# Moving every third VectorE score product to GpSimd, with a longer exponential ring and another rule for TensorE fillers

## The chip, the cores and the metric

The kernel runs on one core of one Trainium2 chip. The metric is the device time of one launch in microseconds. Before the change, five runs had a median of 813.22 us (809.14, 813.22, 813.22, 816.80 and 820.69). All of that is one launch on one core; there is no traffic between cores.

## What is computed

Two attention blocks read the same input and are mixed by a gate. A is a linear attention with a softmax feature map, B is an ordinary softmax attention:

```python
def _A_ref(x, wqkv, w_phi, wo):            # B, S, D = 1, 2048, 512; H = 32; Dh = 16
    q, k, v = heads(x @ wqkv)
    pq = einsum("bhsd,hdf->bhsf", q, w_phi)
    pk = einsum("bhsd,hdf->bhsf", k, w_phi)
    phi_q = concatenate([softmax(pq), softmax(-pq)], -1)
    phi_k = concatenate([softmax(pk), softmax(-pk)], -1)
    kv, z = einsum("bhsf,bhsd->bhfd", phi_k, v), phi_k.sum(2)
    num, den = einsum("bhqf,bhfd->bhqd", phi_q, kv), einsum("bhqf,bhf->bhq", phi_q, z)
    return merge(num / (den[..., None] + 1e-6)) @ wo

def _B_ref(x, wqkv, wo):
    q, k, v = heads(x @ wqkv)
    p = softmax(einsum("bhqd,bhkd->bhqk", q, k) * Dh ** -0.5)
    return merge(einsum("bhqk,bhkd->bhqd", p, v)) @ wo

g = sigmoid((x * gate_w).sum(-1, keepdims=True))
out = g * _A_ref(x, ...) + (1 - g) * _B_ref(x, ...)
```

(`heads` and `merge` stand for the reshapes and transposes of the reference.) Block B needs the exponential of 32 x 2048 x 2048 scores. Cut into tiles of 128 keys by 512 queries, that is 2048 tiles, and nearly everything in this kernel is arranged around them.

## The kernel before, in words

**Tiles and blocks.** A tile is named (b, i, kt): b is one of 32 blocks (four chunks of 512 queries times eight groups of heads), i one of the block's four heads, kt one of sixteen stretches of 128 keys. A score tile is one matmul with a contraction of 32 rows (`qk_mm`); up to four of different heads can lie side by side in the array. Its exponentials multiply the values in another matmul (`pv_mm`) that adds into `psO`, one PSUM bank for the four heads of the block. At a block's end VectorE transposes `psO` (T1), divides by the row sums, and every second block transposes back (T2) into the input of the output projection.

**Two ways to an exponential.** Most tiles go to ScalarE. `slots` pairs them into slots of three and two tiles by turns; slot j is read from one half of `psS` by one ACTIVATE (`add_exp`, line 756) and written to one place of the ring `Ebuf`, which has `ERING = 7` places. The list `DN` says how many tiles of each block go to VectorE instead: 392 of the 2048 before the change, in 98 groups of four. For a group, each tile is computed into a free PSUM bank (`dq`), VectorE converts it to a bit pattern (D1, line 733), then for the whole group of 2048 columns D2 takes the mantissa bits into a buffer m (line 743), D3 the exponent bits into a buffer s (line 745), and D4 multiplies the pattern t by m in place (line 747). TensorE then adds two terms per tile into `psO`, from s and from t (`add_pvd`). The buffers t and s come from small rings (`rings`; before: t has four late ones, x0, x1, a0, a1, s three), and m is a single buffer, so the next group's D2 must wait until this group's product has been read out of m.

**What GpSimd does before.** Apart from setting up masks in the first 14 us, GpSimd only multiplies the feature maps of block A (`phi`, line 946): 32 instructions of 128 x 1024.

**The order.** Nothing is ordered by hand. Every operation is an `Op` with an engine, a duration, a priority and dependencies. `Plan.layout` plays the five engines forward with those durations and at each step gives a free engine the ready operation with the lowest priority number; `Plan.emit` writes each engine's list in that order, with semaphore waits for the dependencies between engines. On the chip each engine follows its list; durations and priorities have no other effect. One rule of the planner matters here: an operation marked `lock` isn't started while a locked operation of the other one of VectorE and GpSimd is under way in the plan (D2, D3, D4, the block-end product and `phi` are locked). That is a rule of the plan alone: no semaphore carries it, so on the chip the two may still overlap if one of them runs late.

**Free banks.** `psM` (bank M) and the sixth bank of `psS` (S5) are lent for one use at a time to projections, `dq` tiles and transposes (`fill`), and come free when the result has been read (`drain`).

**Fillers.** `layout` also puts matmuls without use on TensorE to keep it busy: up to two in front of a score slot (line 688, `op.room`; only where the slot before has three tiles), when a running `debt` exceeds a bound, and single ones into bank M when nothing else is ready (`P.idle`, line 1078).

**Pace of block A.** Its work carries priorities that rise with slot numbers: 76 + 8 per key tile, 210 + 12 per query tile.

Of the kernel before, what the change touches and what calls it, by code (L numbers as in the profile page):

```python
# [10 lines left out]
ALU = mybir.AluOpType  # L11
# [17 lines left out]
DN = (0, 6, 12, 12, 7, 10, 10, 4, 10, 13, 14, 9, 10, 10, 16, 7, 13, 14, 15, 9, 16, 17, 12, 17, 13, 21, 12, 21, 14, 19, 10, 19)  # L29
G_EARLY = 8  # L30
D_FIRST = 12
RIDE = 0.02
PE_CLASS = {"qk": 0, "dq": 0, "pv": 1, "term": 1}
T_PRIO = -10.0
G_DEEP = 5
D_AHEAD = 20.0
CONT = -60.0
ERING = 7
# [5 lines left out]
class Op:  # L44
    __slots__ = ("eng", "dur", "prio", "fn", "deps", "succ", "nd", "ready", "end", "lat", "sem", "count",
                 "name", "full", "extra", "room", "fill", "bank_of", "acq", "rel", "seq", "clock", "take", "pos", "margin", "done", "kind", "heads", "lock")

    def __init__(self, eng, dur, prio, fn, name):
# [7 lines left out]
        self.full, self.extra, self.room, self.fill = 0.0, 0, 0, False  # L56
# [22 lines left out]
class Plan:  # L79
# [3 lines left out]
    def __init__(self):  # L83
        self.ops = []
        self.writer, self.readers = {}, {}
        self.idle, self.rate, self.inslot = None, 0.57, 0.12
# [37 lines left out]
    def layout(self):  # L124
# [14 lines left out]
        debt, debt_t = 0.0, 0.0  # L139
# [3 lines left out]
        while left:  # L143
# [28 lines left out]
            for e in ENGINES:  # L172
# [45 lines left out]
                if e == "pe":  # L218
                    debt, debt_t = min(debt + self.rate * (t - debt_t), 0.5), t
                if pick is None and e == "pe" and self.idle is not None and debt > self.idle[1]:  # L220
                    b, _, fn, after = self.idle
                    if b.free and b.shared and all(x.done for x in after):
                        pick = Op("pe", 0.22, 1e9, fn, "idle")
                        pick.seq, pick.deps, pick.nd = len(self.ops), list(after), 0
                        pick.full = 0.21
                        pick.acq = pick.rel = Fill([b])
                        pick.acq.bank = b
# [12 lines left out]
                if e == "pe":  # L240
                    busy_next = any(o.fill and (o.acq is None or any(b.free and b.shared for b in o.acq.banks))
                                    for _, _, o in queues[e])
                    if op.room and not busy_next and debt > self.inslot and t > 60.0:
                        op.extra = 2 if op.room > 1 and debt > self.inslot + 0.21 else 1
                        op.full += 0.21 * op.extra
                        op.dur += 0.105 + 0.215 * op.extra
                    debt = max(debt - op.full, -0.2)
# [94 lines left out]
def _build(ctx, nc, A_x, A_wqkv, A_w_phi, A_wo, B_wqkv, B_wo, gate_w, out):  # L342
# [23 lines left out]
    Ebuf = sb([128, ERING + 1, 1536], name="E")  # L366
# [145 lines left out]
    def drain(f, mm, eng, dur, prio, fn, reads=(), writes=(), name="", last=True, after=()):  # L512
        op = P.add(eng, dur, prio, lambda e: fn(e, f.ap()), reads=reads, writes=writes, after=[mm] + list(after),
# [9 lines left out]
    kv_mm, va_free = [], []  # L523
# [518 lines left out]
    for t in range(KT):  # L1042
        wp_fill(1, t, 66.0 + t)
# [69 lines left out]
```

## Time and profile before

| What | Value |
| --- | --- |
| median of five runs | 813.22 us |
| the profiled execution's own time | 809.14 us |
| its span, first to last instruction | 807.3 us |
| ScalarE (ACT) busy | 786.4 us, 97% |
| TensorE (PE) busy | 732.1 us, 91% |
| VectorE (DVE) busy | 686.6 us, 85% |
| GpSimd (POOL) busy | 78.1 us, 10% |
| exponentials of block B (line 756) | 663, in two shapes: 331 of 1536 columns, 331 of 1024, one of 512 |
| mean granted TensorE clock | 0.992 |

The shares are averages over the whole span. Busy time of ScalarE counts overlapping records once: an exponential of 1536 columns has a record of 1563 ns and one of 1024 columns a record of 1142 ns, but one follows the other at shorter distance. The VectorE load isn't even. In stretches of 20 us from 60 us on it lies between 10.8 us (200 to 220 us) and 19.8 us (300 to 320 us, 580 to 600 us), and from 440 us to 760 us it is never under 17.1 us.

The profiled execution is the fastest of the five runs; the median lies 4.1 us above it.

### The profile page before, as it was taken

To read this page: it belongs to the slowest core of one execution; us is meant where nothing else is said; L and a number is where in the kernel's file an instruction comes from. 1 tells how busy PE (TensorE), PEld (TensorE's weight loads), DVE (VectorE), ACT (ScalarE), POOL (GpSimd) and SP (SyncE) were. 2 spreads that over 40 slices of the span, in tenths; PEclk is the share of its full clock that TensorE was granted. 3 is DMA by queue.
4 is the path that set the end of the run, shared out by engine and by line. 5 is a ranking of instruction groups with operands and counts; after the bars stand their busy time and mean duration, and the time that the engine had idled before them with its cause. 6 is when DMAs were issued, how large, how long until landed. Compare 5 with 4: busy or idle time off the path is not lost.

```text
span 807.3 us, 13768 instructions
## 1 busy us (share of the span) xinstructions
PE 732.1 (91%) x5821; PEld 232.3 (29%) x5893; DVE 686.6 (85%) x1110; ACT 786.4 (97%) x734; POOL 78.1 (10%) x60
## 2 busy tenths in 40 slices
PE   9899999999998898998899888899898888888999
PEld 4332332333232222233232222222222222222223
DVE  3478877887668999888988999989899999999895
ACT  6999999999999999999999999999999999999995
POOL 5000002132340003000302000000000000000000
PEclk9899999999999999999999999999999999999999
DMA  6600000000100000000000000000000000000000
GB/s 126 137 2 1 1 2 1 1 1 1 53 2 1 1 7 1 7 14 2 1 1 2 1 1 2 1 20 7 1 1 1 1 2 1 1 1 1 20 8 27
DMA packets 18957, 9.29 MB, mean 12 GB/s; under 512 B 13264, under 2 KB 18896, under 8 KB 18896
## 3 DMA queue, kind: packets, MB, share of 16 engines
q1 hardware_dynamic: 17408, 7.74, 4.0%
q8 instruction: 46, 0.75, 0.4%
q10 hardware_dynamic: 1104, 0.66, 0.3%
q0 software_dynamic: 384, 0.02, 0.1%
q14 instruction: 15, 0.12, 0.1%
HBM read 3.69 MB, written 2.10 MB: 7 GB/s over the span
## 4 chain that ended last, share of the span: by engine, by line
ACT 83%; PE 11%; DVE 5%; issue 1%
ACT E_t L756 80%; PE psS L671 3%; ACT EA_t L937 3%; PE psO L769 3%; PE psS L520 2%; PE psM L520 2%; DVE vA_t L733 1%; DVE Tx_t L733 1%; PE psM L440 1%; DVE stat_t L942 1%; DVE vA_t L747 1%; DVE vA_t L745 1%; PE psM L1078 0%; DVE WB_t L743 0%; DVE qz_t L587 0%
## 5 line engine op out<-in xcount | busy, mean ns | idle before, releaser
L756 ACT ACTIVATE E_t<-psS 128x1536 bf16<-128x1536 f32 (+1 forms) x663 | 759.3, 1352 | 6.1 <-PE psS L671 5.0
L671 PE MATMUL psS<-qz_t,kTB_t 32*128 32x512 bf16 x1871 | 284.3, 388 | 53.2 <-ACT E_t L756 42.4
L769 PE MATMUL psO<-E_t,vaug_t 128*32 128x512 bf16 (+1 forms) x1656 | 249.2, 394 | 0.0
L671 PEld LDWEIGHTS psS<-qz_t,kTB_t 32*128 32x128 bf16 x1871 | 70.9, 91 | 272.2 <-ACT E_t L756 209.9
L769 PEld LDWEIGHTS psO<-E_t,vaug_t 128*32 128x32 bf16 (+1 forms) x1656 | 59.0, 93 | 135.5 <-issue 130.4
L733 DVE TENSOR_SCALAR Tx_t<-psS 128x512 int16<-128x512 f32 x118 | 80.5, 682 | 20.0 <-PE psS L671 15.7
L769 PE MATMUL psO<-vA_t,vaug_t 128*32 128x512 bf16 (+1 forms) x384 | 93.3, 391 | 0.0
L671 PE MATMUL psM<-qz_t,kTB_t 32*128 32x512 bf16 x177 | 68.3, 386 | 1.0 <-ACT EA_t L937 0.3
L733 DVE TENSOR_SCALAR Tx_t<-psM 128x512 int16<-128x512 f32 x90 | 61.2, 680 | 9.2 <-PE psM L671 6.0
L733 DVE TENSOR_SCALAR vA_t<-psS 128x512 int16<-128x512 f32 x88 | 60.1, 683 | 10.2 <-PE psS L671 7.6
L769 PE MATMUL psO<-Tx_t,vaug_t 128*32 128x512 bf16 (+1 forms) x208 | 59.5, 386 | 0.0
L946 POOL TENSOR_TENSOR phiQ_t<-EA_t,stat_t 128x1024 bf16<-128x1024 bf16 x16 | 32.9, 2056 | 262.4 <-DVE stat_t L944 251.9
L733 DVE TENSOR_SCALAR vA_t<-psM 128x512 int16<-128x512 f32 x76 | 52.0, 684 | 3.7 <-PE psM L671 2.3
L942 DVE TENSOR_REDUCE stat_t<-EA_t 128x64 f32<-128x1024 bf16 x32 | 38.8, 1213 | 15.7 <-ACT EA_t L937 15.5
L946 POOL TENSOR_TENSOR phiK_t<-EA_t,stat_t 128x1024 bf16<-128x1024 bf16 x16 | 33.3, 2087 | 186.9 <-DVE stat_t L944 179.4
L747 DVE TENSOR_TENSOR Tx_t<-Tx_t,WB_t 128x2048 bf16<-128x2048 bf16 x42 | 50.8, 1209 | 0.1
L747 DVE TENSOR_TENSOR vA_t<-vA_t,WB_t 128x2048 bf16<-128x2048 bf16 x41 | 49.7, 1213 | 0.1
L769 PE MATMUL psO<-WB_t,vaug_t 128*32 128x512 bf16 (+1 forms) x112 | 32.2, 388 | 0.0
L688 PE MATMUL psS<-xT_t,ident_t 128*128 128x512 bf16 x67 | 23.4, 386 | 8.5 <-ACT E_t L756 7.4
L743 DVE TENSOR_SCALAR WB_t<-Tx_t 128x2048 int16<-128x2048 int16 x42 | 29.0, 691 | 0.5
L743 DVE TENSOR_SCALAR WB_t<-vA_t 128x2048 int16<-128x2048 int16 x41 | 28.1, 685 | 0.4
L840 DVE STREAM_TRANSPOSE Tf_t<-psO 128x512 f32<-128x512 f32 x32 | 22.7, 708 | 6.7 <-PE psO L769 6.6
(162 smaller groups left out, 703.8 us busy)
## 6 DMA issues: line engine op xcount, KB each, us to landing
out_dram<-WvA_t SPq DMA_DIRECT2D x14, 128.0 KB, 1.7
WB_t<-in_B_wqkv_dram SPq DMA_DIRECT2D x3, 384.0 KB, 4.7
WvA_t<-in_A_wqkv_dram SPq DMA_DIRECT2D x1, 512.0 KB, 4.1
WoA_t<-in_A_wo_dram SPq DMA_DIRECT2D x1, 512.0 KB, 4.0
WoB_t<-in_B_wo_dram SPq DMA_DIRECT2D x1, 512.0 KB, 5.0
phiK_t<-in_A_x_dram SPq DMA_DIRECT2D x2, 128.0 KB, 2.8
phiK_t<-in_A_x_dram ACTq DMA_DIRECT2D x2, 128.0 KB, 3.0
WB_t<-in_B_wqkv_dram SPq DMA_DIRECT2D x2, 128.0 KB, 4.0
```

What stands on the lines that cost most here:

```text
L520: return [lambda e, ap, i=i: e.matmul(ap, lhsT=lhs[i], rhs=rhs[i], start=(i == 0), stop=(i == len(lhs) - 1)) for i in range(len(lhs))]
L671: return e.matmul(bank, lhsT=kT_B[32 * i:32 * i + 32, hg // 2, 128 * kt:128 * (kt + 1)], rhs=qz[32 * i:32 * i + 32, (b // 8) % 2, hg, :], ...
L688: e.matmul(psS[:, 512 * base:512 * (base + 1)], lhsT=ident[:], rhs=xT[:, 0, 0:NQ], start=True, stop=True)
L733: ops.append(drain(f, mm, "dve", 0.70, d_prio(d), lambda e, ap, q=q: e.tensor_scalar(quarter(t, q).bitcast(I16), ap, EXPB, 0.0, op0=ALU.ad ...
L743: add(0.72, lambda e: e.tensor_scalar(shaped(mi, mi), shaped(ti16, mi), 0x007F, 0x3F00, op0=ALU.bitwise_and, op1=ALU.bitwise_or), tk, [g[" ...
L747: add(1.24, lambda e: e.tensor_tensor(shaped(t, m), shaped(t, m), m, ALU.mult), [g["m"]], tk, "D4")
L756: op = P.add("act", 0.051 + 0.4267 * n, 0.0, lambda e: e.activation(Ebuf[:, j % ERING, 0:512 * n], psS[:, 512 * base:512 * (base + n)], AC ...
L769: return e.matmul(psO[32 * i:32 * i + w, :], lhsT=vaug[:, kt, VW * h:VW * h + w], rhs=rhs, start=start, stop=stop, tile_position=(0, 32 * ...
L840: P.add("dve", 0.69, -50, lambda e: e.transpose(Tf[:, bb, :], psO[:]), reads=["psO"], writes=[("Tf", bb)], after=[pv], name=f"T1.{b}")
L937: ins = e.activation(EA[:, b, :].rearrange("p (g s c) -> p s g c", s=2, c=64)[:, sgn, :, :], ap.rearrange("p (g c) -> p g c", c=64), ACTF. ...
L942: P.add("dve", 1.22, prio, lambda e: e.tensor_reduce(stat[:, b, 1, :], e3, AX.X, ALU.add), reads=[("EA", b)], writes=[("ss", b)], name=f"s ...
L946: P.add("pool", 2.0, prio, lambda e: e.tensor_tensor(dst.rearrange("p (g f) -> p g f", f=DH), e3, stat[:, b, 1, :].unsqueeze(2).to_broadca ...
```

## The change

The product D4 of every third group, 32 of them from group 8 to group 101, is issued on GpSimd as four instructions of 512 columns, each writing its own quarter of t, so that the first terms need only their quarter. All are marked `lock`. The late t buffers become five (n0 added) and the late s buffers four (n1 added); both new ones lie in `WAT`, which is free once the projections of block A's weights are done. The exponential ring gets ten places, as five pairs of 2560 columns. `DN` has another distribution with 416 tiles in 104 groups. The priorities of block A start at 70 and 199 with steps of 8 and 12.5. VectorE's reads of lent banks get at least priority -20, ahead of the group's D2 to D4.

The filler rule changes: TensorE's streaming time over the last 3.4 units of the plan's time is added up, and a filler is put in when its share falls under a bound (0.64 for single ones, which may now use bank S5 too; 0.66 and 0.60 for one or two in a slot; 0.54 for one in a "tight" slot, whose predecessor has only two tiles), from 20 units on rather than 60. The plan's streaming weights of matmuls are raised to the full length for `dq`, the terms and `pv`.

```diff
-DN = (0, 6, 12, 12, 7, 10, 10, 4, 10, 13, 14, 9, 10, 10, 16, 7, 13, 14, 15, 9, 16, 17, 12, 17, 13, 21, 12, 21, 14, 19, 10, 19)
+DN = (0, 8, 10, 13, 11, 9, 13, 11, 3, 11, 7, 11, 13, 15, 18, 6, 15, 14, 18, 10, 15, 17, 20, 12, 17, 15, 16, 20, 16, 18, 17, 17)
+WINDOW = 3.4
+ACTIVE = (0.64, 0.66, 0.60, 0.54)
+K_AT, K_PACE, Q_AT, Q_PACE = 70.0, 8.0, 199.0, 12.5
+POOL_GROUPS = tuple(range(8, 110, 3))
-ERING = 7
+EPAIRS = 5
+ERING = 2 * EPAIRS
...
                 if e == "pe":
-                    debt, debt_t = min(debt + self.rate * (t - debt_t), 0.5), t
-                if pick is None and e == "pe" and self.idle is not None and debt > self.idle[1]:
+                    while streams and streams[0][1] < t - WINDOW:
+                        streams.popleft()
+                    active = sum(y - max(x, t - WINDOW) for x, y in streams) / WINDOW
+                if pick is None and e == "pe" and self.idle is not None and active < ACTIVE[0]:
...
-                    if op.room and not busy_next and debt > self.inslot and t > 60.0:
-                        op.extra = 2 if op.room > 1 and debt > self.inslot + 0.21 else 1
+                    if op.room and t > 20.0 and active < ACTIVE[1]:
+                        op.extra = min(op.room, 1 if active > ACTIVE[2] else 2)
                         op.full += 0.21 * op.extra
                         op.dur += 0.105 + 0.215 * op.extra
-                    debt = max(debt - op.full, -0.2)
+                    elif op.tight and t > 20.0 and active < ACTIVE[3]:
+                        op.extra = 1
+                        op.full += 0.21
+                        op.dur += 0.32
...
-    Ebuf = sb([128, ERING + 1, 1536], name="E")
+    Ebuf = sb([128, EPAIRS, 2560], name="E")
...
-        op = P.add(eng, dur, prio, lambda e: fn(e, f.ap()), ...
+        op = P.add(eng, dur, min(prio, -20.0) if eng == "dve" else prio, lambda e: fn(e, f.ap()), ...
...
-... False: (("x0", "x1", "a0", "a1"), ("w0", "a2", "a3"), "w1")}
+... False: (("x0", "x1", "n0", "a0", "a1"), ("w0", "n1", "a2", "a3"), "w1")}
+    for k in range(2):
+        bufs[f"n{k}"] = (flat(WAT[:, 4 * k:4 * k + 4, :]), wp_ops)
...
-        add(1.24, lambda e: e.tensor_tensor(shaped(t, m), shaped(t, m), m, ALU.mult), [g["m"]], tk, "D4")
+        if g["n"] not in POOL_GROUPS:
+            add(1.24, lambda e: e.tensor_tensor(shaped(t, m), shaped(t, m), m, ALU.mult), [g["m"]], tk, "D4")
+        else:
+            for q in range(4):
+                ops.append(P.add("pool", 1.0, d_prio(g["ts"][0]) - 5.0, lambda e, q=q: e.tensor_tensor(
+                    quarter(t, q), quarter(t, q), quarter(m, q), ALU.mult), reads=[g["m"]], writes=[tk[q]],
+                    name=f"D4{q}.{b}.{kt}"))
+                ops[-1].lock = True
...
-            op.full = 0.05
+            op.full = 0.215
...
-            op.full = 0.21
+            op.full = 0.215 * max(heads.count(i) for i in range(4))
...
-    P.idle = (bM, 0.05, lambda e: e.matmul(psM[:], lhsT=ident[:], rhs=xT[:, 0, 0:NQ], start=True, stop=True), xe)
+    P.idle = ([bM, bS[5]], lambda e, ap: e.matmul(ap, lhsT=ident[:], rhs=xT[:, 0, 0:NQ], start=True, stop=True), xe)
```

## The prediction, made before the changed kernel ran

> **What bounds the kernel now.** I read the busy shares first, then the chain of work that ended last, then the waits of ScalarE alone, then the timeline at the longest of those waits.
>
> ```profile
> PE 732.1 (91%) x5821; PEld 232.3 (29%) x5893; DVE 686.6 (85%) x1110; ACT 786.4 (97%) x734; POOL 78.1 (10%) x60
> ...
> ACT 83%; PE 11%; DVE 5%; issue 1%
> ...
> L756 ACT ACTIVATE E_t<-psS 128x1536 bf16<-128x1536 f32 (+1 forms) x663 | 759.3, 1352 | 6.1 <-PE psS L671 5.0
> ```
>
> ScalarE is busy 97% and is 83% of the chain. The last line (count, busy us and mean ns, idle us just before) says that 663 exponentials waited only 6.1 us in all. The first exponential starts at 10.81 us and the last ends at 797.49 us, 9.8 us before the end. In between, two things can shorten the span: fewer exponentials, and less of the 6.1 us.
>
> Stretches of the chain give the price of an exponential in a row: 72 in 81.51 us from 37.14 us, 45 in 51.07 us from 237.34 us, 30 in 34.16 us from 318.74 us: 166.74 / 147 = 1.134 us, or 2.268 us for a pair of five tiles, 0.454 us a tile.
>
> The waits of the exponentials, one by one in ScalarE's timeline, are 0.31, 0.29 and 0.39 (at 33 to 37 us), 0.21 (170), 1.34 (310), 0.17 (318), 0.20, 0.37, 0.24 (674) and 0.65 (717). The largest:
>
> ```profile
> 306.15 0.63 DVE L743 TENSOR_SCALAR WB_t<-vA_t 128x2048 int16<-128x2048 int16 x1
> 306.70 2.42 DVE L745 TENSOR_SCALAR vA_t<-vA_t 128x2048 int16<-128x2048 int16 x1
> 309.03 0.70 DVE L840 STREAM_TRANSPOSE Tf_t<-psO 128x512 f32<-128x512 f32 x1
> ```
> ```profile
> 306.32 2.25 POOL L946 TENSOR_TENSOR phiQ_t<-EA_t,stat_t 128x1024 bf16<-128x1024 bf16 x1 [0.86 <-DVE stat_t L944]
> ```
> ```profile
> 311.69 1.45 ACT L756 ACTIVATE E_t<-psS 128x1536 bf16<-128x1536 f32 x1 [1.34 <-PE psS L671]
> ```
>
> D3 (line 745; median 0.686 us) took 2.42 us: it ended 0.55 us after GpSimd's product. The block-end transpose and a D1 behind it came late, TensorE waited 1.19 us for that D1, and ScalarE 1.34 us. This is the one place before the change where GpSimd and VectorE visibly cost time, and the change has four times as many such instructions.
>
> Two of the small waits go with the clock:
>
> ```profile
> 668.00:674.00 6.00, 5.46 (x42) 1.12 (x43) 5.26 (x10) 5.62 (x6) 0.00 (x0) 0.72 0.00 0
> ...
> 712.00:718.00 6.00, 5.38 (x42) 1.26 (x40) 5.89 (x11) 5.35 (x6) 0.00 (x0) 0.72 0.00 0
> ```
>
> Columns: length, busy us of PE, PEld, DVE, ACT, POOL with counts, granted clock. 0.72 over 6 us is 3.4 us at half speed. A third such stretch, 6.8 us, lies between 26 and 38 us. The waits beside the three are 0.99 + 0.24 + 0.65 = 1.9 us.
>
> **What the Trainium skill says.** "SBUF — State Buffer", Who interferes with whom: VectorE and GpSimd share a pair of ports as an exclusive lock, taken for the whole instruction by a VectorE instruction in a two-port mode or, against GpSimd's reads, with two SBUF inputs; the other blocks. The trace agrees: the D3 above, and 8 of 32 GpSimd products took 2.11 to 2.79 us instead of 1.93. D1 reads PSUM and isn't concerned. "GPSIMD Engine Reference", 3.1: about 2.6 cycles an element at 1.2 GHz for a two-input product; for 512 columns an estimate of 1.11 us. The trace's 1.93 us for 1024 gives 0.97. "TensorE: Matmul & The Clock Gate", Part 1: low activity over a window of some 3.4 us halves the clock; the 3.4 us stretches agree.
>
> **The change, part by part.**
>
> *Fewer exponentials.* The tiles for VectorE rise from 392 to 416; the built order shows 653 exponentials for 663. 24 tiles x 0.454 = **-10.9 us**, all on the path. The same tiles need their D1 and terms elsewhere.
>
> *VectorE.* D1 goes from 392 to 416, D2 and D3 from 98 to 104 each, D4 from 98 to 72. By the rows (682, 686 and 1213 ns): 24 x 0.682 + 12 x 0.686 - 26 x 1.213 = 16.4 + 8.2 - 31.5 = -6.9 us. VectorE was idle 120 us, so alone this is worth nothing; it keeps the added tiles from overloading the stretches where it is 97 to 99% busy (in 580 to 640 us). The last eight blocks get 136 tiles for 129, 1.75 groups: 1.75 x (4 x 0.682 + 2 x 0.686 + 1.213) = 9.3 us, against some 11 products moved away, 13.3 us.
>
> *GpSimd.* 32 x 4 = 128 quarters. Between 0.97 (trace) and 1.11 us (skill); I take 1.0, so about 128 us more, 206 us in all, 26% busy: no bound. A product takes 4 us instead of 1.2, and s, t and m are held longer. What is queued behind: the next D2 needs m. In the built order 3 to 28 VectorE instructions stand between a GpSimd group's D3 and the next D2, eight or more in 26 of 32 cases, and eight at 0.6 us of issue distance cover 4 us. The terms are the other reader: from the last `dq` of a group to its first t term TensorE's order has 4 to 31 slots before (median 8), and after 5 to 22 for GpSimd groups (median 15), only one under 7 slots, which is 8 us. So the longer product is hidden by terms that come later, which the two added buffers allow. So nothing on the path; were that cover gone, the last `pv` of a block would wait. In GpSimd's own queue a `phi` can now stand behind four quarters, 4 us; before, GpSimd sat idle before nearly every one until VectorE's sums came (251.9 and 179.4 us in all), and its readers come at a pace of 8 to 12.5 slots, 9 to 14 us a tile. The waits of the other queues stay.
>
> *The lock on the chip.* The plan keeps locked operations apart but nothing enforces it. Of 32 products before, 2 blocked a VectorE instruction (by 0.23 and 1.73 us). The same rate makes 8 of 128; a quarter blocks half its length on average, 0.5 us; the wait at 310 us passed 1.34 / 1.73 = 0.77 of a block on. 8 x 0.5 x 0.77 = **+3.0 us**. Bounds: a gain of 1.3 us (the wait at 310 us goes with the new order, no new ones), and for all 128 colliding 49 us.
>
> *Fillers.* In-slot ones go from 103 to 133, single ones from 16 to 28. 42 x 0.217 us (four projection matmuls take 1.04 us, one 0.39) = 9 us of TensorE, which waited for ScalarE 451 times for its next score weights (209.9 us in that row), so it lies beside the exponentials. Only 8 stand in tight slots, whose cover is one exponential of 0.9 us; at most 8 x 0.22 = 1.8 us, taken as nothing. Five pairs stand in the first 5% of TensorE's order, where the long clock stretch was. Gain: between 0 and 1.9 us; I take **-1.9 us**, because the rule measures just the window that the clock seems to follow.
>
> *Ring, priorities, paces.* No exponential waited for a ring place (all waits are on PE score tiles), so ten places gain nothing by themselves and cost nothing; they let `pv` come later. VectorE reading lent banks first makes banks free earlier and D2 to D4 later, covered by the same slots. Block A's paces move 32 products by some ten slots; ScalarE does the same 64 instructions for them. No DMA is added, and SP's queue has the same order. Taken at 0, within 2 us either way.
>
> Sum for the profiled execution: 807.3 - 10.9 + 3.0 - 1.9 = 797.5 us span; with the 1.84 us around it 799.3 us. The median was 4.1 us above the profiled run. If the spread comes from clock stretches, the fillers lessen it; I add half: **801 us**.
>
> **The rivals.**
>
> *Port collisions (ends slower).* Place: D2, D3 and D4 against quarters, above all after 440 us, where VectorE has little idle time and a blocked instruction holds up D1, so a lent bank, so TensorE's fixed order. Each collision costs 0.5 x 0.77 = 0.385 us. To be 1% slower the collisions must bring 821.3 - (811.2 - 10.9 - 1.9) = 22.9 us: 60 of 128 quarters (811.2 is 809.14 and the same half of 4.1). At 70 the time is 798.4 + 27 = 825 us. For it: one long block already cost 1.34 us; drift between plan and chip grows with the GpSimd duration, of which 1.0 is a guess. Against: 2 of 32 before, and quarters are half as long as the old products.
>
> *VectorE or late terms take ScalarE's place (no change).* In 580 to 720 us VectorE is 93 to 99% busy; if the added D1 work and half of the collisions (30 x 0.385 = 11.6 us) show up there, the time is 798.4 + 11.6 = 810 us. For it: waits of VectorE on TensorE and back are spread over dozens of places. Against: work there falls on balance.
>
> *More than the sum.* If nearly all of the 6.1 us go, 811.2 - 10.9 - 6 = 794 us. For it: the terms' distance has doubled. Against: fillers and quarters bring new waits.
>
> **How the numbers follow.** The main case 0.66 (own range 795 to 805), more than the sum 0.10, no change 0.16, collisions 0.08. About 1%, 8 us, is what a measurement can tell: faster than 805.1 us takes the first two, 0.76; same 0.16; slower 0.08. The range 793 to 813 leaves out half of the low case, a third of the no-change case and the slow one.
>
> **What would show it.** Right: 653 exponentials at about 1.13 us each in a row, idle before them near 5 us, GpSimd near 206 us with quarters near 1.0 us, few D2 or D3 records over 0.9 us, no half-clock stretch. Wrong: quarters well over 1.1 us, many D2 to D4 records lengthened, ScalarE idle of 15 us or more, or VectorE waiting before D2 for GpSimd.

## The result, and the profile after

The median over 40 runs of the changed kernel is 807.51 us, against 812.25 us over 77 runs of the kernel before: a ratio of 0.9943, with a 95% interval of 0.9929 to 0.9957. Ratios, and the lines drawn through runs further below, leave out the few runs that take over 1.5% longer than the fastest of their kernel. The sign was right and the time lies in the range, but 801 us had been forecast: 4.7 us were gained where 12 had been promised, and by the prediction's own dividing line, 805.1 us, this is its "no change" case, to which it gave a chance of 0.16. The profiled execution took 806.99 us (span 805.1 us), its span only 2.2 us shorter than the one before, where the sum had promised 9.8.

The page of the changed kernel, the lines that answer to those shown of before: busy time, the granted clock in 40 slices of 20 us, the chain's shares, and three groups of instructions (count, busy us and mean ns of one, then idle us just before and what ended it).

```profile
PE 740.1 (92%) x5890; PEld 229.8 (29%) x5959; DVE 692.4 (86%) x1120; ACT 777.7 (97%) x724; POOL 231.6 (29%) x188
...
PEclk9899999999999999999999999999999999978999
...
ACT 72%; PE 18%; DVE 6%; SPq 2%; issue 1%; POOL 1%; DMA 0%
...
L767 POOL TENSOR_TENSOR Tx_t<-Tx_t,WB_t 128x512 bf16<-128x512 bf16 x44 | 53.7, 1248 | 144.3 <-DVE WAT_t L761 43.9
...
L767 POOL TENSOR_TENSOR vA_t<-vA_t,WB_t 128x512 bf16<-128x512 bf16 x44 | 53.3, 1241 | 122.7 <-DVE WB_t L759 51.2
...
L779 ACT ACTIVATE E_t<-psS 128x1536 bf16<-128x1536 f32 (+1 forms) x653 | 749.8, 1350 | 13.4 <-PE psS L687 10.5
```

The clock line of the kernel before, in the same 40 slices:

```profile
PEclk9899999999999999999999999999999999999999
```

There are 653 exponentials for 663, as built. But they wait 13.4 us instead of 6.1, ScalarE's share of the chain falls from 83 to 72% and TensorE's rises from 11 to 18%. The clock line has a 7 and an 8 at 704 to 745 us, where the line of before has nines.

Where do the waits lie? ScalarE's timeline of the changed kernel (start, length, engine, line, operation, count, and in brackets the wait before):

```profile
391.61 4.62 ACT L779 ACTIVATE E_t<-psS 128x1024 bf16<-128x1024 f32 x4 [1.54 <-PE psS L687]
...
707.55 1.45 ACT L779 ACTIVATE E_t<-psS 128x1536 bf16<-128x1536 f32 x1 [0.54 <-PE psS L687]
709.60 1.02 ACT L779 ACTIVATE E_t<-psS 128x1024 bf16<-128x1024 f32 x1 [0.59 <-PE psS L687]
711.09 2.53 ACT L779 ACTIVATE E_t<-psS 128x1536 bf16<-128x1536 f32 x2 [0.47 <-PE psS L687]
714.13 2.50 ACT L779 ACTIVATE E_t<-psS 128x1536 bf16<-128x1536 f32 x2 [0.51 <-PE psS L687]
717.66 1.45 ACT L779 ACTIVATE E_t<-psS 128x1536 bf16<-128x1536 f32 x1 [1.03 <-PE psS L687]
```

And the same place in windows (length, busy us and count of PE, PEld, DVE, ACT, POOL, then the granted clock, DMA share and GB/s):

```profile
700.00:706.00 6.00, 4.60 (x33) 1.20 (x34) 6.00 (x8) 5.87 (x7) 2.44 (x2) 1.00 0.01 3
706.00:712.00 6.00, 5.49 (x20) 1.13 (x20) 4.62 (x8) 4.39 (x5) 2.87 (x3) 0.70 0.00 0
712.00:718.00 6.00, 6.00 (x30) 0.93 (x27) 5.14 (x9) 4.39 (x5) 0.00 (x0) 0.50 0.00 0
...
736.00:742.00 6.00, 6.00 (x33) 0.96 (x33) 5.08 (x7) 4.33 (x5) 3.90 (x4) 0.50 0.00 0
```

In the stretch at half clock TensorE is busy all the time with few matmuls, and ScalarE is busy 4.3 to 4.4 us of 6 where it was 5.87. Stretches like this add up to 13.7 us in the profiled execution before (beginning at 28, 670 and 714 us) and to 30.7 us after (6.8 at 33, 3.4 at 388, 3.4 at 603, 10.2 at 708, 6.8 at 736 us). The wait of 1.54 us at 391 us belongs to the one at 388: two fillers stand before that slot and take 0.91 us.

The account of the two spans: from the first exponential's start to the last one's end 786.68 us became 784.89. The waits within it rose from 4.4 to 11.3 us; all else fell by 8.7 us. The first exponential starts 0.8 us later, and the time after the last is 1.2 us shorter. So most of the expected gain arrived, and most of it was given back in waits on TensorE; 9.2 of the 11.3 us of waits lie in a half-clock stretch or within 1 us of its end.

The second thing that stands out is the lock. The collision nearest to the long stretch, in VectorE's timeline and then GpSimd's:

```profile
703.40 0.68 DVE L761 TENSOR_SCALAR WAT_t<-vA_t 128x2048 int16<-128x2048 int16 x1
704.01 1.64 DVE L761 TENSOR_SCALAR vA_t<-Tx_t 128x2048 int16<-128x2048 int16 x1
705.57 0.68 DVE L749 TENSOR_SCALAR Tx_t<-psS 128x512 int16<-128x512 f32 x1
```
```profile
703.56 5.31 POOL L767 TENSOR_TENSOR vA_t<-vA_t,WB_t 128x512 bf16<-128x512 bf16 x4 [10.09 <-DVE WB_t L759]
```

The plan had let VectorE run both D3s before the product. On the chip the product waits only for its own m and t; D2 was done, so the first quarter was issued beside the first D3. By the lengths, it took the ports when that D3 ended, and the second D3 needed 1.64 us instead of 0.68. The D1 behind it came a microsecond late and TensorE, at that D1's bank, waited 1.06 us. In the timeline, 24 VectorE records are lengthened like this by more than 0.08 us, together by 15.0 us (27 and 16.0 us with the records that its rows merge); before there were three, 2.1 us.

So there were two theories. **Clock** (F in the expectations, for the fillers): the gain is there, and more half-clock time takes it back, because the new filler rule leaves TensorE too idle. **Lock** (L): the collisions take it back, and the half-clock stretches only follow from them.

### The profile page after: what moved, and what is told of

The parts are those of the page before. It is cut to its first block, busy times and chain, and to the rows that moved or that the text cites. A ratio compares the mean times of both kernels' runs of the same rounds, so it can differ in the third digit from the quotient of the medians.

```text
span 805.1 us, 14035 instructions
## 1 busy us (share of the span) xinstructions
PE 740.1 (92%) x5890; PEld 229.8 (29%) x5959; DVE 692.4 (86%) x1120; ACT 777.7 (97%) x724; POOL 231.6 (29%) x188
## 4 chain that ended last, share of the span: by engine, by line
ACT 72%; PE 18%; DVE 6%; SPq 2%; issue 1%; POOL 1%; DMA 0%
ACT E_t L779 69%; PE psS L687 5%; PE psO L792 5%; ACT EA_t L960 3%; PE psS L534 3%; PE psM L534 2%; SPq L431 2%; PE psS L704 1%; DVE Tx_t L749 1%; DVE vA_t L749 1%; DVE WB_t L759 1%; POOL WAT_t L767 1%; DVE vA_t L761 1%; PE psM L687 0%; DVE Tx_t L764 0%
## 5 line engine op out<-in xcount | busy, mean ns | idle before, releaser
L779 ACT ACTIVATE E_t<-psS 128x1536 bf16<-128x1536 f32 (+1 forms) x653 | 749.8, 1350 | 13.4 <-PE psS L687 10.5
L767 POOL TENSOR_TENSOR Tx_t<-Tx_t,WB_t 128x512 bf16<-128x512 bf16 x44 | 53.7, 1248 | 144.3 <-DVE WAT_t L761 43.9
L767 POOL TENSOR_TENSOR vA_t<-vA_t,WB_t 128x512 bf16<-128x512 bf16 x44 | 53.3, 1241 | 122.7 <-DVE WB_t L759 51.2
L687 PE MATMUL psM<-qz_t,kTB_t 32*128 32x512 bf16 x217 | 84.7, 390 | 2.5 <-DVE Tx_t L749 0.6
L792 PE MATMUL psO<-vA_t,vaug_t 128*32 128x512 bf16 (+1 forms) x304 | 76.4, 389 | 0.0
L749 DVE TENSOR_SCALAR Tx_t<-psS 128x512 int16<-128x512 f32 x85 | 57.9, 681 | 7.1 <-PE psS L687 4.3
L767 POOL TENSOR_TENSOR phiQ_t<-phiQ_t,WoA_t 128x512 bf16<-128x512 bf16 x16 | 18.0, 1153 | 116.7 <-DVE phiQT_t L761 116.7
L767 POOL TENSOR_TENSOR WAT_t<-WAT_t,WB_t 128x512 bf16<-128x512 bf16 x24 | 29.8, 1271 | 64.2 <-DVE WB_t L759 21.6
L704 PE MATMUL psS<-xT_t,ident_t 128*128 128x512 bf16 x101 | 37.0, 408 | 8.9 <-ACT E_t L779 6.7
L792 PE MATMUL psO<-WAT_t,vaug_t 128*32 128x512 bf16 (+1 forms) x156 | 44.1, 402 | 0.0
L764 DVE TENSOR_TENSOR Tx_t<-Tx_t,WB_t 128x2048 bf16<-128x2048 bf16 x24 | 29.1, 1212 | 0.1
```

The costliest lines, as they stand in the source:

```text
L687: return e.matmul(bank, lhsT=kT_B[32 * i:32 * i + 32, hg // 2, 128 * kt:128 * (kt + 1)], rhs=qz[32 * i:32 * i + 32, (b // 8) % 2, hg, :], ...
L704: e.matmul(psS[:, 512 * base:512 * (base + 1)], lhsT=ident[:], rhs=xT[:, 0, 0:NQ], start=True, stop=True)
L749: ops.append(drain(f, mm, "dve", 0.70, d_prio(d), lambda e, ap, q=q: e.tensor_scalar(quarter(t, q).bitcast(I16), ap, EXPB, 0.0, op0=ALU.ad ...
L764: add(1.24, lambda e: e.tensor_tensor(shaped(t, m), shaped(t, m), m, ALU.mult), [g["m"]], tk, "D4")
L767: ops.append(P.add("pool", 1.0, d_prio(g["ts"][0]) - 5.0, lambda e, q=q: e.tensor_tensor(quarter(t, q), quarter(t, q), quarter(m, q), ALU. ...
L779: op = P.add("act", 0.051 + 0.4267 * n, 0.0, lambda e: e.activation(Ebuf[:, j // 2 % EPAIRS, 1536 * (j % 2):1536 * (j % 2) + 512 * n], psS ...
```

## The experiments

### One part at a time, planned anew

e1 leaves the products on VectorE; e2 has the filler rule and streaming weights of before in the changed kernel; e3 plans a quarter at the length that it has on the chip; e4 adds to e3 semaphores that carry the lock in both directions.

```diff
 e1
-POOL_GROUPS = tuple(range(8, 110, 3))
+POOL_GROUPS = ()
 e2
-                    if op.room and t > 20.0 and active < ACTIVE[1]:
-                        op.extra = min(op.room, 1 if active > ACTIVE[2] else 2)
+                    if op.room and not busy_next and debt > self.inslot and t > 60.0:
+                        op.extra = 2 if op.room > 1 and debt > self.inslot + 0.21 else 1
 e3
-                ops.append(P.add("pool", 1.0, d_prio(g["ts"][0]) - 5.0, ...
+                ops.append(P.add("pool", 1.15, d_prio(g["ts"][0]) - 5.0, ...
 e4 (with e3; in layout, where op.lock is set)
+                    other = last_lock["pool" if e == "dve" else "dve"]
+                    if other is not None:
+                        op.deps = op.deps + [other]
+                    last_lock[e] = op
```

> All 104 products on VectorE (POOL_GROUPS empty), everything else as in the changed kernel. Theory L (the products on GpSimd take the shared port from D2/D3 at the wrong moment, the late D1 starves TensorE, its clock halves): lengthened D2/D3 records fall from 24 to about 3, half-clock time from 31 us to 14 us or less, but VectorE gets 39 us more work, so 800 to 808 us. Theory F (the new filler rule leaves TensorE too idle whatever GpSimd does): half-clock time stays near 30 us, idle before the exponentials 11 us or more, 806 us or more. If the move to GpSimd is worth much, over 810 us.

> The changed kernel with the filler rule of before (85 fillers in slots and 39 single ones for 133 and 28). Theory F: half-clock time falls to 14 us or less, idle before the exponentials to about 5 us, 798 to 802 us. Theory L: collisions stay at 20 or more, the half-clock stretches stay or grow with the fewer fillers, 806 to 812 us.

> Only the plan's duration of a quarter is set to what the trace has, 1.15 for 1.0. If collisions come from the plan being too short (theory D): lengthened D2/D3 records fall from 24 to 8 or fewer and the time to 799 to 803 us. Theory L in its stronger form (on the chip GpSimd starts as soon as its inputs are there, before the place the plan gave it, because nothing carries the lock): still 18 or more lengthened records, 804 to 809 us.

> As the run before it, and each locked operation also waits by semaphore for the locked operation of the other engine that the plan put ahead of it, so the chip keeps the plan's order. Theory L: lengthened D2/D3 records 5 or fewer, half-clock time 15 us or less, idle before exponentials 7 us or less, 798 to 803 us. Theory F: collisions gone, half-clock stretches still near 30 us, 805 us or more. If the added waits cost more than the collisions: over 808 us.

| kernel | median us (runs) | ratio to before, 95% | ScalarE idle before exponentials |
| --- | --- | --- | --- |
| e1 | 834.83 (6) | 1.026 [1.022, 1.030] | 35.3 us |
| e2 | 816.56 (22) | 1.006 [1.004, 1.008] | 19.5 us |
| e3 | 837.43 (6) | 1.030 [1.025, 1.035] | 36.6 us |
| e4 | 839.85 (6) | 1.033 [1.029, 1.037] | 43.9 us |

All four are slower than both kernels, even e3, which only tells the planner a truer duration. The wait that does it shows in e1's timeline of ScalarE and in its group of exponentials:

```profile
636.90 3.28 ACT L779 ACTIVATE E_t<-psS 128x1024 bf16<-128x1024 f32 x3 [13.43 <-PE psO L792]
```
```profile
L779 ACT ACTIVATE E_t<-psS 128x1536 bf16<-128x1536 f32 (+1 forms) x653 | 750.5, 1325 | 35.3 <-PE psO L792 25.1
```

A single wait of 13.4 us at a block's end: the products into `psO` are late, which neither kernel has. e3 has such waits too (20.3 us in six), and e2 one of 9.1 us. A changed duration lays out all 14,000 instructions anew. The likely reason for the waits is that the list `DN` fits one plan, so that in the new order some block has more VectorE tiles than it can carry; no run tried a new `DN`, so this isn't shown. Either way these runs price another order, not the part that was edited, and they tell nothing of the theories: e2 and e3 lie above everything that was expected of them, and e1 and e4 meet only an open end ("over 810", "over 808 us"), for another reason than was named there. From here on nearly every edit is made after `P.layout()`, in the order of the changed kernel.

### The lock and the fillers, in the changed kernel's own order

f1 carries the lock by semaphores in both directions, added once an operation has its place, so that the order stays. f2 shortens each quarter to 64 of its 512 columns; it leaves out seven eighths of the 32 products. f3 adds a filler to each roomy slot (one whose predecessor has three tiles) from slot 540 on that has none (43 more). f4 takes all 133 in-slot fillers away.

```diff
 f1 (the lines of e4, with the planned 1.0)
+                    other = last_lock["pool" if e == "dve" else "dve"]
+                    if other is not None:
+                        op.deps = op.deps + [other]
+                    last_lock[e] = op
 f2
-                    quarter(t, q), quarter(t, q), quarter(m, q), ALU.mult), ...
+                    quarter(t, q)[:, 0:64], quarter(t, q)[:, 0:64], quarter(m, q)[:, 0:64], ALU.mult), ...
 f3 (after P.layout())
+    for op in P.order["pe"]:
+        if op.kind == "qk" and op.room and op.extra == 0 and int(op.name[2:]) >= 540:
+            op.extra = 1
 f4 (after P.layout())
+    for op in P.order["pe"]:
+        op.extra = 0
```

> The changed kernel with exactly its own order on each engine; only the plan's order of locked operations is now carried by semaphores between VectorE and GpSimd. Theory L (collisions starve TensorE and set off the half clock): lengthened D2/D3 records none, half-clock time 31 to about 15 us, idle before exponentials 13.4 to 8 us, 800 to 804 us. If VectorE then waits for quarters that last 1.12 us where the plan has 1.0, the waits only change their name: 806 to 812 us. Theory F (fillers too few, whatever the collisions): 805 to 808 us.

> The changed kernel's order, each GpSimd quarter cut to 64 of its 512 columns (seven eighths of these 32 products are left out), so the port is held some 0.2 us. It prices the GpSimd instructions as a whole. Theory L: lengthened records 5 or fewer, only the early half-clock stretch and at most one other, 796 to 801 us. Theory F: half-clock time still 25 us or more, 804 to 808 us.

> The changed kernel's order with one more filler in each empty roomy slot from slot 540 on (43 more), where the longest half-clock stretches lie (707 to 745 us). Theory F: no half-clock stretch after 650 us, 5 us less idle before exponentials, 801 to 803 us. Theory L: the collisions stay, but more streaming may keep the clock; if TensorE's idle of 1 us behind a blocked VectorE is what counts, the stretches stay and the fillers, twice as long there, add waits: 808 to 812 us.

> The changed kernel's order with none of the 133 fillers in slots (28 single ones stay). If fillers hold the clock, half-clock time goes from 31 us to 60 us or more and the time to 815 us or more. If they cost more than they give (those of 0.4 us and more at half clock delay the score tiles), 800 to 806 us.

Half-clock time in the next table is (1 - mean granted clock) x 2 x span, the median over the kernel's runs; for the kernel before, over its runs beside these variants.

| kernel | median us (runs) | ratio to before, 95% | half clock, us | lengthened VectorE records |
| --- | --- | --- | --- | --- |
| before | 812.25 (77) | 1 | 17.8 | 3, 2.1 us |
| after | 807.51 (40) | 0.994 [0.993, 0.996] | 33.8 | 24, 15.0 us |
| f1 | 811.05 (22) | 0.999 [0.997, 1.001] | 43.7 | 0 |
| f2 | 803.84 (6) | 0.989 [0.983, 0.994] | 28.9 | 7, 3.1 us |
| f3 | 808.66 (22) | 0.995 [0.993, 0.997] | 27.4 | 22, 13.3 us |
| f4 | 817.36 (22) | 1.005 [1.002, 1.008] | 102.8 | 23, 14.4 us |

**The lock.** f1 has not one lengthened record and is no faster than after: VectorE now waits for GpSimd by semaphore, some 16 us in all, as long as it was blocked before. That was the expectation for waits that only change their name. f2 takes most of GpSimd's added work away (it is busy 116.6 us for 231.6; a shortened quarter still takes 0.30 us), so it estimates what the collisions and the long quarters cost together: 807.5 - 803.8 = 3.7 us by the medians. This is no sharp bound, as its six runs lie between 800.2 and 804.9 us and 7 lengthened records remain; and part of it is clock, since half-clock time is 5 us less. f2's time falls between the ranges of the two theories, its half-clock time into F's.

**The fillers.** Without them half-clock time is three times as long and the time 9.9 us longer. With 43 more, the stretches after 650 us are gone, as the windows of f3 show at the places shown above of the changed kernel:

```profile
700.00:706.00 6.00, 5.62 (x43) 1.47 (x39) 6.00 (x10) 6.00 (x7) 0.34 (x1) 1.00 0.01 3
706.00:712.00 6.00, 5.05 (x28) 1.26 (x27) 5.53 (x9) 5.34 (x5) 4.97 (x4) 1.00 0.00 0
712.00:718.00 6.00, 5.67 (x43) 1.59 (x43) 5.87 (x11) 6.00 (x7) 0.00 (x0) 1.00 0.00 0
...
736.00:742.00 6.00, 5.89 (x60) 1.58 (x59) 6.00 (x7) 5.92 (x6) 4.50 (x4) 1.00 0.01 3
```

The clock stays at 1.00, and ScalarE is busy 5.3 to 6.0 us there instead of 4.3 to 4.4. That is what theory F expected, but not its 801 to 803 us: f3 isn't faster than after, so the fillers themselves cost as much as the clock gives.

### More fillers, and smaller pieces

g1 gives single fillers to every roomy slot from 300 on and none before slot 40 (214 in all); g2 issues each quarter as two instructions of 256 columns; g3 does both; g4 deals fillers out as g1 does in the kernel before (199 for 103).

```diff
 g1, and g4 in the kernel before (after P.layout())
+    for op in P.order["pe"]:
+        if op.kind == "qk":
+            j = int(op.name[2:])
+            op.extra = 0 if j < 40 else 1 if op.room and j >= 300 else min(op.extra, 1)
 g2
+                    [e.tensor_tensor(quarter(t, q)[:, c:c + 256], quarter(t, q)[:, c:c + 256],
+                     quarter(m, q)[:, c:c + 256], ALU.mult) for c in (0, 256)][-1]
```

> The changed kernel's order with its slot fillers dealt anew: none before slot 40, never two in one slot, one in every roomy slot from slot 300 on (214 for 133). If pairs inside a half-clock stretch are what costs (early waits of 2.05 us and 1.54 us at 391 us): early waits near 1.1 us, the one at 391 us near 0.4 us, half-clock time under 20 us, 802 to 805 us. If the clock is already paid for and streaming only delays score tiles: 808 to 812 us.

> The changed kernel's order, each quarter issued as two instructions of 256 columns, the same result. Theory L: as many lengthened VectorE records (about 24), but each block at most some 0.6 us for 1.1, their sum 15 to 7 or 8 us, 804 to 806 us. If GpSimd takes the port again before VectorE gets it, the sum stays near 15 us and the time at 807 us or more, as each instruction has its own start-up.

> Both edits. If collisions and fillers act through different waits, the gains add: 800 to 803 us, idle before exponentials under 8 us. If both only keep the clock up, the sum is that of the better one alone: 803 to 806 us.

> The kernel before in its own order with the same dealing of fillers (199 for 103 in slots). If half-clock stretches explain why its runs scatter upward from 808.6 us (theory F applied to it): no stretch after 50 us, median 808 to 810 us, ratio 0.995 to 0.998. If not: ratio 0.999 or more.

g1 took 814.38 us (22 runs; 1.002 [1.000, 1.004]) at 34.1 us of half clock, g2 812.42 (22; 0.999 [0.996, 1.001]) at 40.5, g3 810.83 (22; 0.997 [0.995, 0.999]) at 27.5, g4 828.53 (6; 1.020 [1.016, 1.023]) at 34.7. None is faster than the changed kernel; g1 and g3 lie above all that was expected of them. 96 more fillers, with half-clock time up by 17 us all the same, cost the kernel before 16 us (g4), and g1's 81 more fillers bought no clock at all (34.1 us for 33.8).

g2 was meant to halve a collision. The number of lengthened records stayed (26), their sum fell only to 11.3 us where 7 or 8 was expected, and the pieces aren't half as long. Groups of g2 and of the changed kernel by shape (least, median and greatest ns of one):

```profile
L767 POOL TENSOR_TENSOR Tx_t<-Tx_t,WB_t x88: 658/668/1208, 280.8 to 783.4; 128x256 bf16<-128x256 bf16 x88
```
```profile
L767 POOL TENSOR_TENSOR Tx_t<-Tx_t,WB_t x44: 1145/1156/1686, 281.3 to 775.3; 128x512 bf16<-128x512 bf16 x44
```

Two halves take 1.34 us for 1.16, so GpSimd is busy 251.6 us instead of 231.6.

### The clock's price, and each part in the kernel before

h1 puts the new filler rule alone into the kernel before, h4 the products of 30 of its 98 groups on GpSimd with the two added buffers and nothing else (both planned anew); h2 keeps after's order with at most one filler to a slot and none before slot 40 (90 left); h3 makes only GpSimd wait for the locked VectorE operation that the plan puts before it.

```diff
 h2 (after P.layout())
+    for op in P.order["pe"]:
+        if op.kind == "qk":
+            op.extra = 0 if int(op.name[2:]) < 40 else min(op.extra, 1)
 h3 (in layout, where op.lock is set)
+                    if e == "pool" and last_lock["dve"] is not None:
+                        op.deps = op.deps + [last_lock["dve"]]
+                    last_lock[e] = op
 h4 (in the kernel before)
+POOL_GROUPS = tuple(range(8, 98, 3))
...
+        if g["n"] not in POOL_GROUPS:
+            ...
+        else:
+            for q in range(4):
+                ops.append(P.add("pool", 1.0, d_prio(g["ts"][0]) - 5.0, ...
```

(h1's edit is the hunk of the rule and of the weights in the change itself, with the ring and `DN` of before.)

In the expectations, "the line's start" is the time that the straight line of a kernel's time against its half-clock time gives at no half clock (drawn below under "The clock's price").

> The kernel before with only the new filler rule (191 fillers in slots and 14 single ones for 103 and 16; the plan is laid out anew). If the rule is what fails: half-clock time stays at 18 us or rises, each added filler costs about 0.06 us of the line's start (805.9 to 811 us), median 814 to 820 us. If the rule holds the clock and the other parts of the change lose it: half-clock time 10 us or less, median 808 to 812 us.

> The changed kernel's order with no filler before slot 40 and never two in one slot (90 for 133). If pairs inside half-clock stretches cost more than they hold: the line's start falls from 798.4 to 795 or 796 us, half-clock time 35 to 45 us, median 804 to 808 us. If they hold the clock: half-clock time over 55 us, 810 us or more.

> The changed kernel's order; GpSimd's locked instructions wait for the VectorE one that the plan put ahead, VectorE waits for nothing new. If GpSimd's starting ahead of its place is what blocks VectorE: lengthened records 24 to 12 or fewer, half-clock time from 34 to 28 us, the line's start near 797 us, median 803 to 806 us. If they come from quarters lasting 1.12 us where the plan has 1.0, as many are lengthened, 807 to 811 us.

> The kernel before with only the product of every third group (30 of 98) on GpSimd in quarters and the two added buffers; same tiles on ScalarE, fillers by the old rule. No exponential fewer, so no gain is expected: the line's start 807 to 812 us (collisions +3), half-clock time from 18 to 25 us if collisions lose the clock, median 812 to 820 us. If VectorE's load held back ScalarE before, it is faster: under 809 us.

h1 took 849.0 us (6 runs; 1.044 [1.038, 1.049]), far over its expectations, and waits 27.2 us on `psO`, as e1 does. h4 took 813.48 us (22; 1.001 [0.998, 1.003]), as expected: products on GpSimd without more tiles on VectorE don't change the time, though VectorE's busy time falls to 661.9 us. h2 took 808.61 us (22; 0.997 [0.995, 0.999]); its 51.6 us of half clock lie between the two expectations, and its line starts at 792.6 us, under the 795 or 796 of the first.

h3 took 804.54 us (9; 0.992 [0.988, 0.996]), with its line's start at 795.4 us, as expected if GpSimd's early start is what blocks VectorE; but 17 records stay lengthened, where 12 or fewer had been expected. Its profiled execution is one of its slower ones (809.23 us with 41.7 us of half clock, where its median run has 27.3). The timelines at the collision shown above, VectorE and then GpSimd:

```profile
704.73 0.68 DVE L765 TENSOR_SCALAR WAT_t<-vA_t 128x2048 int16<-128x2048 int16 x1
705.34 0.68 DVE L765 TENSOR_SCALAR vA_t<-Tx_t 128x2048 int16<-128x2048 int16 x1
705.94 0.68 DVE L753 TENSOR_SCALAR Tx_t<-psS 128x512 int16<-128x512 f32 x1
```
```profile
706.10 4.48 POOL L771 TENSOR_TENSOR vA_t<-vA_t,WB_t 128x512 bf16<-128x512 bf16 x4 [9.67 <-DVE vA_t L765]
```

GpSimd now starts behind both D3s and no record is lengthened here. But a half-clock stretch of 6.8 us begins at 710 us all the same:

```profile
708.00:714.00 6.00, 6.00 (x22) 1.17 (x22) 4.41 (x8) 5.22 (x6) 2.58 (x3) 0.64 0.00 0
```

So that stretch doesn't need the collision. Nor does its length: i1, further below, has no lengthened record there either, and 10.2 us of half clock from 709 us. In both, TensorE was busy 91% of the 3.4 us before the stretch, so a pause of TensorE doesn't explain it there. Nor does the collision suffice: in f3 the same D3 took 1.64 us too, and with the added fillers the clock stayed full. f1 and f2, where next to nothing collides there, haven't got the stretch either, so it doesn't follow from one thing alone. The lock theory in its strong form, that the stretches only follow from the collisions, falls.

**The clock's price.** The mean granted clock is recorded for every run, so a run's time can be set against its half-clock time, and a straight line drawn through the runs of one kernel. In the kernel before (203 runs, 9.7 to 44.2 us of half clock, correlation 0.97) the line is 805.8 us + 0.33 us for each us of half clock; in the changed kernel (54 runs, i2 below included, 27.3 to 51.8 us, correlation 0.89) it is 797.8 us + 0.285 for each. At 30 us, which lies in both ranges, they give 815.6 and 806.3 us: **the changed kernel is 9.3 us faster at equal half-clock time**. And the median rose from 17.8 to 33.8 us, 16 us, which at 0.3 us each takes 5 us back. (That half-clock time is the cause of the added time, and not a sign of it, is read from runs of one and the same program; f4 agrees, where more of it goes with 9.9 us more in spite of fewer fillers.)

The same lines give a rough price of the fillers, with everything else in one order. The five kernels differ in the fillers' places too, not in their number alone. "At 30 us" is read off each kernel's own line; h2's runs begin at 40 us and f4's at 86 us, so their values are stretched beyond their runs, f4's far beyond.

| in-slot fillers | kernel | median us | half clock, us | at 30 us of half clock |
| --- | --- | --- | --- | --- |
| 0 | f4 | 817.4 | 102.8 | 793 to 795 |
| 90 | h2 | 808.6 | 51.6 | 802.0 |
| 133 | after | 807.5 | 33.8 | 806.3 |
| 176 | f3 | 808.7 | 27.4 | 810.2 |
| 214 | g1 | 814.4 | 34.1 | 813.4 |

Read down the last column, a filler costs about 0.1 us ((813.4 - 802.0) / 124 = 0.09); g4 against the kernel before agrees (826.7 - 815.6 = 11.1 us for 96, 0.12 each). What it buys shrinks: from 0 to 133 fillers 69 us of half clock, 0.52 each, worth 0.16 us; from 133 to 176 only 6.4 us, 0.15 each, worth 0.045. So by this estimate the gain and the price are about equal near 133, and the median is flat from 90 to 176.

### Both mended, and the kernel after again

i1 is h3 without the ten fillers before slot 40; i2 is the changed kernel once more beside it.

```diff
 i1 (h3, and after P.layout())
+    for op in P.order["pe"]:
+        if op.kind == "qk" and int(op.name[2:]) < 40:
+            op.extra = 0
```

> h3 without the ten fillers before slot 40. If the early fillers only lengthen the score tiles in a stretch of half clock that comes anyway: early waits 2.05 to 1.1 us, the line's start 795.4 to 794.4 us, median 802 to 805 us, below the changed kernel beside it. If they shorten that stretch: half-clock time up by 3.4 us and no gain, 804 to 807 us.

> The changed kernel itself on the same chip, for comparison: 806 to 809 us, half-clock time about 34 us, line's start near 798 us.

i1 took 805.87 us (6 runs; 0.993 [0.990, 0.995]), i2 807.97 (13; 0.995 [0.993, 0.997]). The waits of the exponentials up to 41 us, not counting the first exponential's, fell to 0.94 us as meant (after: 2.19, before: 0.99), but the first stretch lasted 10.2 us for the 6.8 of after, and another came at 330 us, so the end is no nearer. The time is that of the second expectation; its reason isn't shown, for the first stretch lasts 10.2 us in the profiles of f1, f2, f3 and h3 too, which keep those fillers. i2 came out as expected. Apart from f2 with its shortened products, h3 and i1 have the lowest medians, but their intervals overlap with that of after: that they beat it isn't shown.

## Why the prediction was right in sign and wrong in size

**Fewer exponentials, -10.9 us: right, and a little too large.** The exponentials' busy time fell from 759.3 to 749.8 us, 9.5 us, and the profiled pair gives -8.7 us outside the waits. The prediction without its clock term is -10.9 + 3.0 = -7.9 us; the two lines above give -9.3 at equal half clock. Term by term these don't fit closely: at 0.1 us each the 30 added slot fillers cost some 3 us, which the prediction put at nothing and the -9.3 contains, so something else must be better than it was taken to be. What, no run shows.

**The cover by VectorE and GpSimd: right, with wrong durations.** Neither became the bound and no block end waits in the changed kernel. But a quarter is 1.15 us when nothing blocks it (four in a row took 4.48 us in h3, 1.12 each), not the 1.0 that I took. The Trainium skill, "GPSIMD Engine Reference", 3.1, gave an estimate of 1.11; the 0.97 that I scaled from `phi`, a product with another pair of operands, was the worse guide. With the collisions GpSimd is busy 231.6 us, not 206, and D2's waits for it stay small (1.4 us in all). VectorE was to fall to 679.7 us and rose to 692.4; the 15.0 us of lengthened records account for that.

**The lock, +3.0 us: about the size, from wrong factors.** Not 8 records and 4 us but 24 and 15.0 us; not 0.77 of it is passed on but some 0.3 by f2's medians, which cut 11.9 us of lengthening and 3.7 us of time, with other GpSimd work and some half clock in the same 3.7. The one wait at 310 us from which I took 0.77 was a bad sample of one. The step that said that nothing enforces the plan's lock was right, and the trace agrees with the Trainium skill, "SBUF — State Buffer", Who interferes with whom, that the other engine is held for a whole instruction: D3 took 1.64 us for 0.68. But the rate of 2 in 32 could not be carried over. The likely reason, which no run tests by itself: the old products met VectorE by chance; the new ones start just when D2 of their own group is done, that is, when the next locked VectorE operation is due.

**The fillers, -1.9 us "because the rule measures just the window that the clock seems to follow": this step failed.** Half-clock time didn't vanish but went from 17.8 to 33.8 us, which is +5 us. The rule reckons with planned times, and the chip's times are others. Just before the stretch at 708 us TensorE waited 1.06 us for the late D1, and in the 3.4 us before it was busy 2.14 us, 63%. In the plan the share at the two score slots that fall there was 0.69 and 0.63, above the bounds that hold for them (0.66 and 0.54), so it called for no filler. Nor does a busy TensorE always hold the clock, for h3's stretch came after 91% busy. Whether other bounds in the rule would have done better isn't tested. And fillers don't "lie beside the exponentials" for nothing: each costs about 0.1 us at equal half clock, and takes more than twice as much TensorE time at half clock (0.52 us for 0.217). Of the five early pairs, which I had down as a gain, the last two run in the first half-clock stretch (the two of one pair take 1.03 us there), and the early waits went from 0.99 to 2.19 us.

Added up roughly: clock +5 for -1.9 is 7 us worse; the rest, -9.3 for -7.9, is 1.4 better; the base that I took, 811.2 us, was 1 us under the median of 77 runs. 801 + 7 - 1.4 + 1 = 807.6 us. This must close, since the lines come from the same runs; it shows where the miss lies, and isn't a second proof.

**The rivals.** Collisions cost about what the sum had set aside for them, 3.7 for 3.0 us, and so don't explain the miss by themselves. "VectorE or late terms" didn't come as described: no exponential waits on a block's end, though the time is near its 810 us. "More than the sum" fell with the waits of 13.4 us.

**Open.** What part of the change doubled the half-clock time isn't settled. GpSimd's products in the kernel before bring some 6 us of it (h4: 24.3 for 17.8, in an order laid out anew), and shortening them in the changed kernel takes away 5 (f2: 28.9 for 33.8). For the other 10 us or so, more tiles on VectorE, the order that came of the new plan with its ring and paces, and the filler rule remain; the runs that changed the rule alone were laid out anew (e2, h1) and can't separate them.

## What to carry to other kernels

Where a planner deals out the work, test a part with the order frozen: telling this planner the true length of one instruction cost 30 us, probably because another list was fitted to the old plan. When a bound engine gets less work, look at the clock of the engine that feeds it, before and after: here half the gain was lost to it, although TensorE is only 18% of the chain. And give fillers a price; here each cost more than the clock that it bought from about 133 on.

## What the runs showed of the hardware that wasn't expected

Half-clock time costs much less than it lasts: 0.28 to 0.33 us for each us in these two kernels, where ScalarE is the bound. It also doesn't need a long pause. The 3.4 us before the two long stretches of the changed kernel:

```profile
705.02:708.43 3.41, 2.14 (x11) 0.50 (x9) 3.27 (x6) 2.87 (x3) 3.41 (x4) 1.00 0.00 0
732.33:735.74 3.41, 1.73 (x17) 0.36 (x12) 3.41 (x7) 3.41 (x4) 0.00 (x0) 1.00 0.00 0
```

TensorE was busy 63% and 51%, with no pause over 1.1 us. The Trainium skill, "TensorE: Matmul & The Clock Gate", Part 1, lets the clock follow how busy TensorE has been, and names an idle window of about this length for the fall to half rate. Here the windows weren't idle, and the measured shares decide.

All 20 traces together show more. In each, every half-clock stretch begins on one grid of 3.413 us and lasts whole steps of it (but for a last one that the program's end cuts off), and the grid lies elsewhere in each execution: the stretches of i2 begin 1.2 us sooner after the program's start than the same ones of after. From 60 us on, until 20 us before the end, the step after one at full clock was at half clock in 29 of 37 cases where TensorE had been busy under 65% of the step, in 66 of 633 at 65 to 85%, and in 5 of 3416 above. So whether a pause is caught may hang on how the grid falls, which would fit the spread of half-clock time between runs of one kernel; no run tests this. Busy time isn't all of it either, as the five show, among them the stretches of h3 and i1 at 710 and 709 us.

To make one engine wait by semaphore for the port costs no less than to let it be blocked, if both wait for each other (f1: 811.05 us, 16 us of waits in place of 15 us of lengthened records). When only GpSimd waits, which is busy 27% of the time, lengthened records fall to 17 and 7.6 us (h3), and the median is 804.54 us.
